# Block sums of k as two more columns of its transposing products, the last output tile in two halves, and a new listing: block-sparse attention followed by an MLP-mixer

## The chip, the core and the metric

The kernel runs on one NeuronCore of a Trainium2 chip. The core has a matrix engine (TensorE, PE; its weight loads are shown apart as PEld), a vector engine (VectorE, DVE), an activation engine (ScalarE, ACT), a general engine (GpSimd, POOL) and a queue engine that issues transfers (SyncE, SP). Each engine takes its instructions strictly in the order in which they are listed, and waits where an input or a buffer isn't ready. The metric is the device time of one execution in microseconds; the median of several runs counts.

## The reference

```python
# q, k, v: (4, 8, 768, 64); block = 64, n_blocks = 12, top_k = 3
k_rep = k.reshape(B, H, n_blocks, block, D).mean(axis=3)
gate_scores = np.einsum('bhsd,bhnd->bhsn', q, k_rep)
gate_scores = np.where(causal, gate_scores, -1e9)     # causal by blocks
top_idx = np.argsort(gate_scores, axis=-1)[..., -top_k:]
# a query attends to the blocks in top_idx and to its own, causally
scores = scale * np.matmul(q, k.transpose(0, 1, 3, 2))
attn = softmax(np.where(mask, scores, -1e9))
x = np.matmul(attn, v)                                # heads side by side: (4, 768, 512)
# the mixer, x as (batch, token, channel)
h = np.maximum(x.T @ w_tok1, 0.0) @ w_tok2            # along the tokens, 768 -> 256 -> 768
u = x + h.T
out = u + np.maximum(u @ w_ch1, 0.0) @ w_ch2          # along the channels, 512 -> 1536 -> 512
```

Which three blocks a query takes depends on comparisons of gate scores, so these are computed more exactly than the rest, which is in 16 bits.

## The kernel before, in words

The 32 heads are handled as 16 pairs, 0 to 15; four pairs make a batch. `pair(p)` writes down the steps of one pair, `mlp(b)` those of a batch's channel MLP. No step is issued there: each goes into a planner (`Plan`) with its engines and estimated costs, the buffers that it reads and writes, and a due time `pr`, made of the pair's start and a constant of the table `L` (lines 46 to 51). `Plan.run` then lists the steps for each engine, always taking the ready step with the earliest due time, chooses between engines where a step may run on two, and assigns ring buffers; that listing is what the engines follow. Where it sees PE idle before the first MLP, it puts in products of zeros (`fill`, L766).

Steps of a pair, with their lines:

- k, q and v are loaded by SP (L472, L477) into rings of three buffers each.
- k's six tiles of 128 keys x two heads are transposed on PE in f32, by products with the identity `id32` (`transposed`, L419), in two halves of three tiles, each into one of four PSUM tiles `pm`. ACT or DVE copies them in f16 to KA (`kev`, L496).
- Block sums of k: pairs 0 to 3 take them with a reduction on DVE over the transposed half in PSUM (L487), which leaves six sums per half; a product with `side` (L491) spreads them into `ks2`, the two heads apart. Pairs 4 to 7 reduce in the same way and split the sums in three bf16 parts (L433, L436). Pairs 8 to 15 transpose k in f16 (L508) and get the sums from a separate load of k (`block_sums`, L444, L449).
- q is transposed likewise and copied to QT (`qev`), and from there cast to QA on one of three engines.
- The gate: PE multiplies q with the sums, in f32 for pairs 0 to 3 (L543), in bf16 parts for the others (L559, L526, L552). DVE adds the causal bias (L546, L564), finds the third largest of each row (L573, L575), compares (L576) and masks the own block (L579) into `bn`. For pairs 0 to 4 PE transposes these bits (L598) and ACT or DVE copies them into QA's last 12 rows; for pairs 5 to 15 DVE transposes them (L584) and four transfers on SP carry them there (L587).
- Scores (L619): QA against KA, whose last 12 rows hold the block indices, so that the mask comes out of the product itself. The scores go into two PSUM tiles `sc`, in three pieces per head; ACT takes the exponential (L626), POOL cuts the diagonal blocks (L634), PE multiplies with v (L643), DVE divides (L646, L650).
- The mixer along the tokens: L661, a rectification, L675, an addition on DVE (L678), a transpose to uT (L686 and copies).

The channel MLP of a batch runs in two halves of 384 tokens: 12 groups of four products (`ch1`, L704) with a rectification each (L710 on ACT or L712 on DVE), then three output tiles of 128 tokens x 512 channels, 12 products each (`ch2`, L721), an addition on DVE (L724) and a write of 256 KB by SP (L727). Its products stand between the attention steps of later batches.

Of the kernel before, what the change touches and what calls it, by code (L numbers as in the profile page):

```python
# [9 lines left out]
FP = mybir.dt.float32  # L10
# [3 lines left out]
ALU = mybir.AluOpType  # L14
AX = mybir.AxisListType
# [9 lines left out]
def _layout():  # L25
    col, diag, width = {}, [], []
    for g, banks in enumerate(GROUPS):
        mine, w = [], 0
        for bk, pieces in enumerate(banks):
# [13 lines left out]
COL, DIAG, WIDTH = _layout()  # L43

EARLYP = 8
EARLY, PACE = 5.58, 13.33
L = dict(kd=28.57, qd=25.92, vd=11.57, va=-8.52, kt=12.35, kr=17.84, ke=-10.79, qt=15.5, qe=4.07, q16=14.86, g=19.74,
         b=14.78, k16=23.05, kx=14.61, kc=15.1, r=24.94, kb=35.09, ks=47.26, w1=2.86, w2=-1.57, wc1=17.92, wc2=28.28,
         tok=9.0, ml=12.54, o0=-0.3, o1=1.07, o2=2.31, o3=0.96, o4=-4.5, o5=1.61, o6=-2.0, o7=-4.89, o8=-4.68,
         o9=0.71, o10=0.86, o11=-1.11, o12=-2.65, o13=-2.86, o14=1.45, o15=0.65, m0=-2.18, m1=-0.36, m2=-0.52,  # L50
         m3=-1.94, th=3.11, bd=4.29)


class Ring:
# [187 lines left out]
def dve(n, rate=0.96):  # L242
    return {"DVE": (n / rate + 70.0, n / rate + 155.0)}
# [15 lines left out]
def kernel(  # L259
# [33 lines left out]
    def sb(shape, dt, name):  # L293
        return sp.tile(shape, dt, tag=name, name=name)
# [4 lines left out]
    def copy(e, out, in_):  # L299
        if e is nc.scalar:  # L300
            e.copy(out=out, in_=in_)  # L301
        else:
            e.tensor_copy(out=out, in_=in_)  # L303

    P = Plan()
    ENG = {"PE": nc.tensor, "ACT": nc.scalar, "DVE": nc.vector, "POOL": nc.gpsimd, "SP": nc.sync}
# [19 lines left out]
    w1 = sb([128, NJ, DT], F16, "w1")  # L326
# [28 lines left out]
    nc.vector.memset(zero, 0.0)  # L355
    nc.gpsimd.memset(id32, 0.0)
    nc.gpsimd.affine_select(out=id32, in_=id32, pattern=[[-1, 128]], compare_op=ALU.not_equal, fill=1.0, base=0, channel_multiplier=1)
    nc.gpsimd.memset(ind, MASKV)
    nc.gpsimd.affine_select(out=ind, in_=ind, pattern=[[1, S]], compare_op=ALU.is_ge, fill=0.0, base=0, channel_multiplier=-64)
    nc.gpsimd.affine_select(out=ind, in_=ind, pattern=[[-1, S]], compare_op=ALU.is_ge, fill=0.0, base=63, channel_multiplier=64)  # L360
# [56 lines left out]
    def transposed(src, i, t):  # L417
        for j in range(3):
            nc.tensor.transpose(out=t[:, 128 * j:128 * j + 128], in_=src.t[:, 3 * i + j].rearrange("p x d -> p (x d)"), identity=id32)  # L419

    def halves(i):
        return slice(HS * i, HS * i + HS)
# [38 lines left out]
    def pair(p):  # L461
# [2 lines left out]
        step = T(p + 1) - T(p)  # L464
        t0 = T(p) + L[f"o{p}"]
        early, thirds = p < FIRST, p >= L["th"]
        q32, k32, v32 = Buf(q32r), Buf(k32r), Buf(v32r)
        qs, ks_, vs = q[b, h:h + 2], k[b, h:h + 2], v[b, h:h + 2]
        QA, KA, VA, QT = Buf(QAr), Buf(KAr), Buf(VAr), Buf(QTr)
# [11 lines left out]
        if early:  # L481
            ks2b = kp = Buf(kppr if thirds else ksr)
            ks3 = Buf(ks3r) if thirds else None
            for i in range(2):
                t = Buf(Rr)
                P.op(pe(slow=3), lambda t=t, i=i: transposed(k32, i, t.t), rd=[(k32, 0), (k32, 1)], wr=[(t, 0)], pr=t0 - L["kt"])
                P.op(dve(HS), lambda t=t, i=i: nc.vector.tensor_reduce(  # L487
                    out=ks3.t[:, 0, 6 * i:6 * i + 6] if thirds else t.t[:, HS:HS + 6], in_=t.t[:, 0:HS].rearrange("c (n w) -> c n w", w=64),
                    axis=AX.X, op=ALU.add), rd=[(t, 0)], wr=[(ks3, i) if thirds else (t, 1)], pr=t0 - L["kr"])
                if not thirds:  # L490
                    P.op({"DVE": (150.0, 220.0)}, lambda t=t, i=i: nc.vector.tensor_tensor(  # L491
                        out=ks2b.t[:, :, 6 * i:6 * i + 6], in0=t.t[:, HS:HS + 6].rearrange("c (o n) -> c o n", o=1).broadcast_to([128, 2, 6]),
                        in1=side, op=ALU.mult), rd=[(t, 1)], wr=[(ks2b, i)], pr=t0 - L["kr"] + 0.1)
                for x in range(2):
                    def kev(e, t=t, i=i, x=x):
                        copy(ENG[e], KA.t[0:64, x, halves(i)], t.t[64 * x:64 * x + 64, 0:HS])  # L496
                    P.op({**dve(HS), **act(HS)}, kev, rd=[(t, 0)], wr=[(KA, (x, i))], pr=t0 - L["ke"])
            if thirds:
                split(ks3, lambda x: kp.t[64 * x:64 * x + 64, :, x, :], lambda h, x: h[64 * x:64 * x + 64], [(ks3, 0), (ks3, 1)], kp, t0 - L["kr"] + 0.1)
        else:  # L500
            k16 = Buf(k16r)
            P.op({"POOL": (840.0, 880.0)}, lambda: nc.gpsimd.tensor_copy(
                out=k16.t, in_=k32.t.rearrange("p j x d -> p j (x d)")), rd=[(k32, 0), (k32, 1)], wr=[(k16, 0)], pr=t0 - L["k16"])
            t = Buf(Rr)

            def ktr(t=t):
                for j in range(NJ):
                    nc.tensor.transpose(out=t.t.bitcast(F16)[:, 128 * j:128 * j + 128], in_=k16.t[:, j, :], identity=id16)  # L508
            P.op(pe(*[128] * NJ), ktr, rd=[(k16, 0)], wr=[(t, 0)], pr=t0 - L["kt"])
            for x in range(2):  # L510
                def kev(e, t=t, x=x):
                    copy(ENG[e], KA.t[0:64, x, :], t.t.bitcast(F16)[64 * x:64 * x + 64, 0:S])
                P.op({"DVE": (530.0, 610.0), **act(S)}, kev, rd=[(t, 0)], wr=[(KA, (x, 0)), (KA, (x, 1))], pr=t0 - L["ke"])
# [58 lines left out]
                for x in range(2):  # L572
                    nc.vector.max(out=m8.t[:, j, x, :], in_=gm.t[:, j, NB * x:NB * x + NB])  # L573
        P.op({"DVE": (730.0, 820.0)}, top, rd=[(gm, 0)], wr=[(m8, 0)], pr=t0 - L["g"] + 0.2)
        P.op({"DVE": (140.0, 210.0)}, lambda: nc.vector.tensor_copy(out=third(), in_=m8.t[:, :, :, 2:3]), rd=[(m8, 0)], wr=[(g, 1)], pr=t0 - L["g"] + 0.25)  # L575
        P.op({"DVE": (220.0, 300.0)}, lambda: nc.vector.tensor_tensor(  # L576
            out=below(), in0=gm.t.rearrange("p j (x n) -> p j x n", n=NB), in1=third().broadcast_to([128, NJ - 1, 2, NB]), op=ALU.is_lt),
            rd=[(gm, 0), (g, 1)], wr=[(g, 0)], pr=t0 - L["g"] + 0.3)
# [114 lines left out]
    def mlp(b):  # L693
        u, uT = u_of[b], uT_of[b]
        t0, span = T(PPB * (b + 1)) + L["ml"] + L[f"m{b}"], PACE * PPB
        n = 0
        for i in range(2):
            h2 = Buf(h2r)
            for f in range(NFC):
                m = Buf(Rr, "mlp")  # L700

                def ch1(f=f, i=i, m=m):
                    for c in range(NCC):
                        nc.tensor.matmul(out=m.t[:, 0:HS], lhsT=wc1[:, c, 128 * f:128 * f + 128], rhs=uT.t[:, c, HS * i:HS * i + HS],  # L704
                                         start=(c == 0), stop=(c == NCC - 1))
                P.op(pe(*[HS] * NCC), ch1, rd=[(uT, (c, i)) for c in range(NCC)] + [W["wc1", c] for c in range(NCC)], wr=[(m, 0)], pr=t0 + span * n / 48)

                def relu(e, f=f, m=m, h2=h2):
                    if e == "ACT":
                        nc.scalar.activation(out=h2.t[:, f, :], in_=m.t[:, 0:HS], func=AF.Relu)  # L710
                    else:
                        nc.vector.tensor_scalar(out=h2.t[:, f, :], in0=m.t[:, 0:HS], scalar1=0.0, scalar2=None, op0=ALU.max)  # L712
                P.op({**act(HS), **dve(HS)}, relu, rd=[(m, 0)], wr=[(h2, f)], pr=t0 + span * n / 48 + 0.05)
                n += 1
            for jj in range(3):
                j = 3 * i + jj
                m, o = Buf(Rr, "mlp"), Buf(osr)
                for s in range(4):
                    def ch2(jj=jj, s=s, m=m, h2=h2):
                        for f in range(3 * s, 3 * s + 3):  # L720
                            nc.tensor.matmul(out=m.t, lhsT=h2.t[:, f, 128 * jj:128 * jj + 128], rhs=wc2[:, f, :], start=(f == 0), stop=(f == NFC - 1))  # L721
                    P.op(pe(*[DM] * 3), ch2, rd=[(h2, f) for f in range(3 * s, 3 * s + 3)] + [W["wc2", 3 * s]], wr=[(m, 0)], pr=t0 + span * n / 48)
                    n += 1
                P.op(dve(DM), lambda j=j, m=m, o=o: nc.vector.tensor_tensor(  # L724
                    out=o.t.rearrange("p (c d) -> p c d", d=128), in0=u.t[:, :, j, :], in1=m.t.rearrange("p (c d) -> p c d", d=128), op=ALU.add),
                    rd=[(m, 0)] + [(u, (c, i)) for c in range(NCC)], wr=[(o, 0)], pr=t0 + span * n / 48 + 0.05)
                P.op({"SP": (600.0, 1500.0, 700.0)}, lambda j=j, o=o: nc.sync.dma_start(out=out[b, 128 * j:128 * j + 128, :], in_=o.t),  # L727
                     rd=[(o, 0)], wr=[(o, 0)], pr=t0 + span * n / 48 + 0.06)

    for b in range(B):  # L730
        if b * PPB >= FIRST:
# [78 lines left out]
```

## Time and profile before

| what | value |
|---|---|
| three runs | 264.1, 264.17, 264.48 us; median 264.17 |
| profiled execution | 264.49 us, of which 262.8 us are the span from the first to the last instruction |
| busy PE, PEld | 250.4 us (95%), 172.1 us (65%) |
| busy DVE, ACT, POOL | 157.3 us (60%), 167.1 us (64%), 120.0 us (46%) |
| granted clock of TensorE | 0.998 |
| moved by DMA | 33.21 MB |

A busy time is the union of an engine's instructions; a product's end is modelled, so products that overlap in the pipeline count once. In a row of the timeline or the chain stand the start in us, the duration in us, the engine, the line, and what is written from what; "x6" is a run of six. In a row of groups stand the count, the busy time in us and the mean of one in ns, then the idle time before them and what ended it. In a row by stage stands the stretch, then per engine the busy time and the number of instructions, the granted clock, the mean busy share of the DMA engines and GB/s.

### The profile page before, as it was taken

To read this page: it belongs to the slowest core of one execution; us is meant where nothing else is said; L and a number is where in the kernel's file an instruction comes from. 1 tells how busy PE (TensorE), PEld (TensorE's weight loads), DVE (VectorE), ACT (ScalarE), POOL (GpSimd) and SP (SyncE) were. 2 spreads that over 40 slices of the span, in tenths; PEclk is the share of its full clock that TensorE was granted. 3 is DMA by queue.
4 is the path that set the end of the run, shared out by engine and by line. 5 is a ranking of instruction groups with operands and counts; after the bars stand their busy time and mean duration, and the time that the engine had idled before them with its cause. 6 is when DMAs were issued, how large, how long until landed. Compare 5 with 4: busy or idle time off the path is not lost.

```text
span 262.8 us, 6757 instructions
## 1 busy us (share of the span) xinstructions
PE 250.4 (95%) x2585; PEld 172.1 (65%) x2585; DVE 157.3 (60%) x527; ACT 167.1 (64%) x265; POOL 120.0 (46%) x222
## 2 busy tenths in 40 slices
PE   7689999988999999999999999999999999999994
PEld 7566688775667677666776677657665665554541
DVE  5788997998368475786684767638574452301103
ACT  2689989975776683459974968457765661360520
POOL 8136884963256898666993807133132110000000
PEclk9999999999999999999999999999999999999999
DMA  8999997689998799943997940021002100212103
GB/s 165 224 211 215 231 221 148 102 139 146 179 269 139 190 246 220 241 85 126 213 219 158 216 114 2 8 80 42 7 2 75 54 0 2 80 40 80 44 0 120
DMA packets 88960, 33.21 MB, mean 126 GB/s; under 512 B 82464, under 2 KB 85152, under 8 KB 88736
## 3 DMA queue, kind: packets, MB, share of 16 engines
q1 hardware_dynamic: 83984, 28.33, 50.0%
q0 software_dynamic: 3232, 3.93, 9.8%
q10 hardware_dynamic: 1712, 0.52, 1.0%
q8 instruction: 20, 0.33, 0.5%
q14 instruction: 12, 0.10, 0.1%
HBM read 30.01 MB, written 6.29 MB: 138 GB/s over the span
## 4 chain that ended last, share of the span: by engine, by line
PE 83%; DVE 6%; DMA 4%; ACT 2%; issue 2%; SPq 1%; DVEq 0%; ACTq 0%
PE pm L704 20%; PE pm L721 18%; PE sc L619 12%; PE pm L643 7%; PE sc L721 5%; PE pm L419 4%; PE pm L661 4%; PE pm L675 3%; PE sc L704 3%; PE pm L559 2%; DMA k<-in_k_dram 2%; DMA QA<-bnt 2%; PE pm L686 2%; ACT E L626 1%; PE pm L508 1%
## 5 line engine op out<-in xcount | busy, mean ns | idle before, releaser
L626 ACT ACTIVATE E<-sc 128x1024 f16<-128x1024 f32 (+1 forms) x96 | 83.7, 918 | 13.8 <-PE sc L619 12.7
L634 POOL TENSOR_SCALAR_AFFINE_SELECT E<-E 128x256 f16<-128x256 f16 x96 | 38.8, 409 | 69.1 <-ACT E L626 68.6
L704 PE MATMUL pm<-uT,wc 128*128 128x384 f16 x340 | 64.3, 326 | 0.0
L721 PE MATMUL pm<-wc,h 128*128 128x512 f16 x228 | 59.2, 379 | 0.0
L704 PEld LDWEIGHTS <-wc 128*128 128x128 f16 x384 | 36.2, 98 | 23.2 <-issue 0.6
L619 PE MATMUL sc<-QA,KA 76*128 76x512 f16 (+3 forms) x256 | 49.0, 305 | 2.0 <-DMA QA<-bnt 1.1
L710 ACT ACTIVATE h<-pm 128x384 f16<-128x384 f32 x60 | 29.5, 492 | 20.9 <-PE pm L704 20.7
L721 PEld LDWEIGHTS <-h 128*128 128x128 f16 x288 | 26.6, 98 | 23.3 <-issue 1.0
L619 PEld LDWEIGHTS <-KA 76*128 76x128 f16 x256 | 22.8, 98 | 16.7 <-issue 2.9
L643 PEld LDWEIGHTS <-E 128*128 128x128 f16 x672 | 25.1, 98 | 4.9 <-issue 1.1
L643 PE MATMUL pm<-VA,E 128*128 128x65 f16 x651 | 25.5, 193 | 1.0 <-ACT uT L301 0.9
L724 DVE TENSOR_TENSOR os<-u,pm 128x512 f32<-128x512 f16 x19 | 12.9, 681 | 20.5 <-PE pm L721 19.1
L712 DVE TENSOR_SCALAR h<-pm 128x384 f16<-128x384 f32 x25 | 13.9, 555 | 13.1 <-PE pm L704 12.7
L449 POOL TENSOR_TENSOR kb<-kb 96x512 f32<-96x512 f32 (+2 forms) x18 | 20.0, 1114 | 0.0
L303 POOL CAST QA<-QT 64x768 f16<-64x768 f32 x12 | 9.8, 819 | 20.7 <-ACT QT L301 18.7
L724 DVE TENSOR_TENSOR os<-u,sc 128x512 f32<-128x512 f16 x5 | 3.3, 686 | 26.0 <-PE sc L721 26.0
L650 DVE TENSOR_TENSOR x<-pm,rc 128x384 f16<-128x384 f32 x31 | 17.2, 556 | 0.8
L678 DVE TENSOR_TENSOR u<-x,pm 128x384 f16<-128x384 f16 x30 | 15.5, 547 | 2.7 <-PE pm L675 2.5
L301 ACT COPY uT<-pm 128x384 f16<-128x384 f16 x21 | 9.1, 486 | 12.5 <-PE pm L686 12.5
L301 ACT COPY QT<-pm 128x384 f32<-128x384 f32 x24 | 11.0, 485 | 8.0 <-PE pm L419 7.8
L552 POOL TENSOR_TENSOR R<-R 128x640 bf16<-128x640 f32 x12 | 15.0, 1252 | 1.9 <-DVE R L526 0.9
L419 PE MATMUL pm<-id,q 128*128 128x128 f32 x96 | 14.6, 276 | 1.0 <-ACT QT L301 1.0
(90 smaller groups left out, 358.0 us busy)
## 6 DMA issues: line engine op xcount, KB each, us to landing
k<-in_k_dram SPq DMA_DIRECT2D x32, 192.0 KB
v<-in_v_dram SPq DMA_DIRECT2D x16, 384.0 KB
out_dram<-os SPq DMA_DIRECT2D x24, 256.0 KB
q<-in_q_dram SPq DMA_DIRECT2D x30, 192.0 KB
wc<-in_moe_w_ch_dram POOLq DMA_DIRECT2D x8, 384.0 KB, 6.3
kb<-in_k_dram SPq DMA_DIRECT2D x2, 1536.0 KB
w<-in_moe_w_tok_dram POOLq DMA_DIRECT2D x2, 384.0 KB, 6.2
QA<-bnt SPq DMA_DIRECT2D x44, 9.0 KB
```

Source lines behind the costliest of these rows:

```text
L301: e.copy(out=out, in_=in_)
L419: nc.tensor.transpose(out=t[:, 128 * j:128 * j + 128], in_=src.t[:, 3 * i + j].rearrange("p x d -> p (x d)"), identity=id32)
L449: P.op({"POOL": (step * 2.15 + 60, step * 2.15 + 140)}, lambda n=n, o=o, step=step: nc.gpsimd.tensor_tensor(out=kb.t[:, o:o + step] if n > ...
L619: nc.tensor.matmul(out=s.t[:, at:at + 128 * m], lhsT=KA.t[:, x, 128 * kk:128 * kk + 128], rhs=QA.t[:, q0:q0 + m, x, :], start=True, stop=True)
L626: nc.scalar.activation(out=E.t[:, 1024 * g_:1024 * g_ + WIDTH[g_]], in_=s.t[:, 0:WIDTH[g_]], func=AF.Exp, scale=scale)
L634: nc.gpsimd.affine_select(out=o, in_=o, pattern=[[0, 2], [1, 128]], compare_op=ALU.is_ge, fill=0.0, base=0, channel_multiplier=-1)
L643: nc.tensor.matmul(out=t[:, jq, :], lhsT=E.t[:, cc:cc + 128], rhs=VA.t[:, x, kk, :], start=(kk == 0), stop=(kk == jq))
L650: P.op(dve(384), lambda a=a, rc=rc, x=x: nc.vector.tensor_tensor(out=xp.t[:, :, 64 * x:64 * x + 64], in0=a.t[:, 0:NJ * 65].rearrange("p (j ...
L704: nc.tensor.matmul(out=m.t[:, 0:HS], lhsT=wc1[:, c, 128 * f:128 * f + 128], rhs=uT.t[:, c, HS * i:HS * i + HS], start=(c == 0), stop=(c == ...
L710: nc.scalar.activation(out=h2.t[:, f, :], in_=m.t[:, 0:HS], func=AF.Relu)
L721: nc.tensor.matmul(out=m.t, lhsT=h2.t[:, f, 128 * jj:128 * jj + 128], rhs=wc2[:, f, :], start=(f == 0), stop=(f == NFC - 1))
L724: P.op(dve(DM), lambda j=j, m=m, o=o: nc.vector.tensor_tensor(out=o.t.rearrange("p (c d) -> p c d", d=128), in0=u.t[:, :, j, :], in1=m.t.r ...
```

## The change

Three things. First, for pairs 0 to 3 the identity gets two more columns, ones in the upper and in the lower 64 rows (`idk`, 128 x 130, set up on POOL). k's tiles are multiplied with it by ordinary f32 products, so that each tile of 128 keys comes out transposed with its two block sums beside it, and the reductions fall away; the product with `side` reads the sums from their columns. Pairs 4 to 7 keep the reductions. Second, the last output tile of the last batch is made in two halves of 256 channels, each with its own products, addition and write. Third, the table `L` and `PACE` have new values, so that the planner lists everything anew.

```diff
-EARLY, PACE = 5.58, 13.33
+EARLY, PACE = 5.58, 12.85
...
+    idk = sb([128, 130], FP, "idk")
+    nc.gpsimd.memset(idk, 0.0)
+    nc.gpsimd.affine_select(out=idk[:, 0:128], in_=idk[:, 0:128], pattern=[[-1, 128]], compare_op=ALU.not_equal, fill=1.0, base=0, channel_multiplier=1)
+    for x in range(2):
+        nc.gpsimd.memset(idk[64 * x:64 * x + 64, 128 + x:129 + x], 1.0)
...
+        sums = p < L["sm"] and not thirds
...
+                if sums:
+                    def turned(t=t, i=i):
+                        for j in range(3):
+                            nc.tensor.matmul(out=t.t[:, 130 * j:130 * j + 130], lhsT=k32.t[:, 3 * i + j].rearrange("p x d -> p (x d)"), rhs=idk, start=True, stop=True)
+                    P.op(pe(slow=6), turned, rd=[(k32, 0), (k32, 1)], wr=[(t, 0)], pr=t0 - L["kt"])
                     P.op({"DVE": (150.0, 220.0)}, lambda t=t, i=i: nc.vector.tensor_tensor(
-                        out=ks2b.t[:, :, 6 * i:6 * i + 6], in0=t.t[:, HS:HS + 6].rearrange("c (o n) -> c o n", o=1).broadcast_to([128, 2, 6]),
-                        in1=side, op=ALU.mult), rd=[(t, 1)], wr=[(ks2b, i)], pr=t0 - L["kr"] + 0.1)
+                        out=ks2b.t[:, :, 6 * i:6 * i + 6].rearrange("c x (j n) -> c x j n", n=2),
+                        in0=t.t[:, 0:390].rearrange("c (o j w) -> c o j w", o=1, w=130)[:, :, :, 128:130].broadcast_to([128, 2, 3, 2]),
+                        in1=side.rearrange("c x (j n) -> c x j n", n=2), op=ALU.mult), rd=[(t, 0)], wr=[(ks2b, i)], pr=t0 - L["kr"])
...
-                m, o = Buf(Rr, "mlp"), Buf(osr)
+                o = Buf(osr)
+                wide = DM // 2 if b == B - 1 and j == NJ - 1 else DM
+                for w in range(0, DM, wide):
+                    m = Buf(Rr, "mlp")
...
```

The copies to KA read the transposed tiles at a stride of 130 columns for these pairs. In the new listing there is more that differs: on SP the loads of k for pair 3 stand ahead of v for pair 0, and those of k for pair 4 ahead of q for pair 2; the bits of pair 5 are transposed sooner behind their gate; ten groups of `ch1` for seven stand ahead of pair 5's scores; and for pairs 12 to 15 less of PE's other work stands between a pair's gate and its first scores.

More of the change, by code (lines that the diff above doesn't have):

```diff
@@ L494, in pair @@
                 for x in range(2):
                     def kev(e, t=t, i=i, x=x):
-                        copy(ENG[e], KA.t[0:64, x, halves(i)], t.t[64 * x:64 * x + 64, 0:HS])
+                        a = t.t[64 * x:64 * x + 64]
+                        copy(ENG[e], KA.t[0:64, x, halves(i)].rearrange("d (j w) -> d j w", w=128),
+                             a[:, 0:390].rearrange("d (j w) -> d j w", w=130)[:, :, 0:128] if sums else a[:, 0:HS].rearrange("d (j w) -> d j w", w=128))
                     P.op({**dve(HS), **act(HS)}, kev, rd=[(t, 0)], wr=[(KA, (x, i))], pr=t0 - L["ke"])
@@ L574, in pair @@
         P.op({"DVE": (730.0, 820.0)}, top, rd=[(gm, 0)], wr=[(m8, 0)], pr=t0 - L["g"] + 0.2)
-        P.op({"DVE": (140.0, 210.0)}, lambda: nc.vector.tensor_copy(out=third(), in_=m8.t[:, :, :, 2:3]), rd=[(m8, 0)], wr=[(g, 1)], pr=t0 - L["g"] + 0.25)
+        P.op({"DVE": (165.0, 240.0)}, lambda: nc.vector.tensor_copy(out=third(), in_=m8.t[:, :, :, 2:3]), rd=[(m8, 0)], wr=[(g, 1)], pr=t0 - L["g"] + 0.25)
         P.op({"DVE": (220.0, 300.0)}, lambda: nc.vector.tensor_tensor(
@@ L716, in mlp @@
                 j = 3 * i + jj
-                m, o = Buf(Rr, "mlp"), Buf(osr)
[L718 to L728, printed above, removed]
+                o = Buf(osr)
```

38 lines of the change are left out of this document (28 added, 10 removed).

## The prediction

> **What bounds the kernel now.** I read the busy time by stage first, then the chain that ended last, then the timelines of VectorE (DVE) and TensorE (PE) in the first stage, then single groups.
>
> ```profile
> core 0: us, PE busy (x) PEld busy (x) DVE busy (x) ACT busy (x) POOL busy (x), PEclk, DMA share, GB/s
> 6.40:59.00 52.60, 47.23 (x632) 38.76 (x633) 45.98 (x177) 46.33 (x72) 31.84 (x63) 1.00 1.04 187
> 59.00:65.20 6.20, 5.11 (x49) 3.25 (x48) 5.50 (x23) 2.96 (x7) 2.42 (x7) 1.00 1.01 141
> 65.20:215.00 149.80, 149.80 (x1595) 102.32 (x1594) 93.26 (x304) 102.17 (x157) 79.49 (x133) 1.00 0.59 127
> 215.00:262.80 47.80, 43.56 (x267) 23.15 (x264) 8.89 (x15) 14.17 (x30) 0.81 (x2) 0.99 0.14 50
> ```
>
> From 65.2 to 215 us PE has no idle time at all: that stage is bound by PE's own work, and PE does the same work there in either kernel. What can change lies elsewhere: 5.4 us (52.60 - 47.23) of PE idleness up to 59 us, where PE, ACT and DVE are each near 90% busy and wait for one another; 1.1 us (6.20 - 5.11) behind it; and the end after PE's last product.
>
> ```profile
> 20.40 1.03 PE pm L543 x10
> ...
> 22.38 0.68 PE pm L419 x6
> ...
> 59.47 4.73 DMA QA<-bnt
> 64.33 1.03 PE sc L619 x6
> ...
> 259.08 0.69 DVE os L724
> ```
>
> These are rows of the chain: start, time, what. Pair 5's scores (L619) at 64.33 wait for a transfer of gate bits that was issued from 56.29 on; that is the 1.1 us. At the end one addition on DVE of 0.69 us stands behind the last product, and a write of 256 KB behind it.
>
> **The block sums, in the first stage.** Removed: eight DVE reductions, two per pair of pairs 0 to 3.
>
> ```profile
> L487 DVE TENSOR_REDUCE pm<-pm 128x6 f32<-128x384 f32 x8 | 4.5, 558 | 0.9 <-PE pm L419 0.8
> L543 PE MATMUL pm<-ks,QT 128*128 128x24 f32 x40 | 4.9, 264 | 1.2 <-DVE ks L491 1.2
> L543 PEld LDWEIGHTS pm<-ks,QT 128*128 128x128 f32 x40 | 4.8, 192 | 1.6 <-ACT QT L301 1.5
> L365 POOL MEMSET side<- 64x6 f32 x2 | 0.5, 273 | 0.1
> L357 POOL TENSOR_SCALAR_AFFINE_SELECT id<-id 128x128 f32<-128x128 f32 x1 | 0.3, 292 | 0.1
> ```
>
> The 24 transposes of k become 24 ordinary f32 products with 130 columns. A transposing step costs 113 ns (0.68 us for 6, chain). No row shows the new one. From below: the gate's f32 product, which the trace records in two parts, takes 206 ns (1.03 us for 5) with only 24 columns; two parts of a transpose's length make 226 ns. From above: if the gate's 206 is weight loading that can't hide behind the columns, 226 + 206 = 432 ns. I take 226, since loads overlap with products elsewhere in this trace (PEld is busy beside PE in every stage). That adds 24 x 0.113 = 2.7 us to PE's work, all before 25 us.
>
> The Trainium skill ("FP8 and Floating Point Precision", TensorE Precision Notes) says that a true FP32 product makes four passes through the array; with 130 columns at the 2.4 GHz of its page "TensorE: Matmul & The Clock Gate" that is an estimate of 217 ns, 0.2 us less in the sum; the trace's 206 ns at 24 columns doesn't fall with the columns as four passes would, so it speaks for loading as the floor there.
>
> What the reductions cost where they stand:
>
> ```profile
> 3.85 2.68 DVE L379 COPY KA<-ind 12x768 f16<-12x768 f16 x6 [1.72 <-POOL ind L360]
> ...
> 10.63 0.28 DVE L546 TENSOR_TENSOR gm<-pm,cst 128x120 f32<-128x120 f32 x1 [0.92 <-issue]
> 10.95 0.82 DVE L573 MAX8 m<-gm 128x8 f32<-128x12 f32 x10
> 11.68 0.55 DVE L487 TENSOR_REDUCE pm<-pm 128x6 f32<-128x384 f32 x1
> 12.14 0.17 DVE L575 COPY pm<-m 128x10 f32<-128x10 f32 x1
> 12.22 0.56 DVE L487 TENSOR_REDUCE pm<-pm 128x6 f32<-128x384 f32 x1
> 12.68 0.28 DVE L576 TENSOR_TENSOR pm<-gm,pm 128x120 f32<-128x120 f32 x1
> ...
> 13.06 0.28 DVE L579 TENSOR_TENSOR bn<-pm,cst 128x120 f16<-128x120 f32 x1
> ...
> 14.15 1.00 DVE L303 COPY QA<-pm 12x640 f16<-12x640 f16 x2 [0.33 <-PE pm L598]
> 16.86 3.66 ACT L626 ACTIVATE E<-sc 128x1024 f16<-128x1024 f32 x4
> ```
>
> Two of them, 0.46 us each from start to start, sit in pair 0's own gate chain. I walked the new listing by hand: each instruction starts when its engine is free and its inputs are there, 0.2 us after a PE group for the engine that evicts it, 0.05 us otherwise, with these durations. Pair 0's gate product stays at 9.25: its k products end 0.7 us later (six at 0.226 for six at 0.113) and push q's transposes, which cancels the reductions saved ahead of the gate. The setup of the 130-column identity puts about 1 us on POOL ahead of the index rows (a select like the old identity's, 0.29, a memset no longer than that, and two memsets at 0.27), and so the KA copies on DVE, which wait for those rows, end near 7.5 for 6.53 (3.85 + 2.68); DVE's first new input comes at 7.96, so this is hidden; with that cover gone it costs up to 1 us. Then pair 0's bits are done at 12.5 for 13.3, its QA rows at 14.2 for 15.15, its first exponential starts at 15.95 for 16.86.
>
> **The new listing of the first stage** gives part of this back and takes it again later. The loads of k for pair 3 go ahead of q for pair 2 on SP's queue, and of v for pair 0.
>
> ```profile
> 16.22 0.49 PE L419 MATMUL pm<-id,q 128*128 128x128 f32 x3
> ...
> 20.24 1.19 PE L543 MATMUL pm<-ks,QT 128*128 128x24 f32 x10
> ...
> 59.01 1.46 PE L704 MATMUL pm<-uT,wc 128*128 128x384 f16 x8
> 56.29 3.95 SPq L587 DMA_DIRECT2D QA<-bnt  x4
> ```
>
> Pair 2's q is transposed at 16.22 now; in the walk it waits for a PSUM tile until 21.4, and its gate comes at 24.4 for 20.24. Queued behind it on PE stand pair 1's second scores, for which ACT waits: the thirteenth exponential starts 1.0 us later than now. Behind it the order is better: the thirtieth ends at 52.55, the gate bits of pair 5 leave DVE without two evictions between them (their transfer is issued at 54.7 for 56.29), and the first MLP product, ahead of which both listings put the same PE work, starts at 58.05 for 59.01. I take -0.9 us. Bounds: the walk's own worst lag is 1.6 us (the twenty-first exponential), so +1.6 at the least favourable; at best PE's 5.4 us of idleness swallow the 2.7 us of new work and vanish, -2.7.
>
> **59 to 65 us.** Ten groups of L704 stand ahead of pair 5's scores for seven. The bits landed 64.33 - 56.29 = 8.0 us after the first issue; issued at 54.7 they land at 62.7, and the scores are due at 65.4: the wait of 1.1 us goes, -1.1. If the transfer is slower by 2.7 us it comes back; it can't gain more.
>
> **65 to 215 us.** There is no idleness to win, only to lose. Per pair the chain is: gate product, DVE steps, bnt transposed, four issues on SP, landing, scores. PE must have other work as long as this takes.
>
> ```profile
> 181.25 0.23 PE L559 MATMUL pm<-ksp,R 128*128 128x72 bf16 x2
> 184.60 0.57 DVE L584 STREAM_TRANSPOSE bnt<-bn 128x384 f16<-128x384 f16 x1
> 185.23 3.31 SPq L587 DMA_DIRECT2D QA<-bnt  x4
> 189.00:189.50 0.50, 0.50 (x6) 0.30 (x4) 0.41 (x1) 0.29 (x1) 0.00 (x0) 1.00 0.16 19
> 189.50:190.00 0.50, 0.50 (x6) 0.48 (x5) 0.00 (x0) 0.34 (x2) 0.00 (x0) 1.00 0.00 0
> 194.45 0.23 PE L559 MATMUL pm<-ksp,R 128*128 128x72 bf16 x2
> 198.17 0.58 DVE L584 STREAM_TRANSPOSE bnt<-bn 128x384 f16<-128x384 f16 x1
> 205.51 0.60 PE L619 MATMUL sc<-QA,KA 76*128 76x512 f16 x3
> ```
>
> Here it takes 3.3 us to bnt, 0.6 to the issue, 4.3 until the last packets stopped (189.5): 8.2 us; for the next pair 3.7 + 0.6 + 4.3 = 8.6, and its scores come at 205.51, 11.0 us behind its gate, without a wait. Counting the work listed between gate and first scores at the rows' paces, pairs 12 to 15 have 11.3, 11.2, 11.0 and 11.0 us now, and 8.3, 8.2, 7.8 and 9.3 in the new listing. With 8.2 us PE waits 0.4 in all, with 8.6 it waits 0.3 + 0.4 + 0.8 = 1.5. I take +0.7; from below nothing, from above as in the second rival.
>
> **The last tile in halves.** PE's work is the same columns in twice as many products.
>
> ```profile
> 259.80:260.50 0.70, 0.00 (x0) 0.00 (x0) 0.00 (x0) 0.00 (x0) 0.00 (x0) 1.00 0.00 0
> 260.50:261.50 1.00, 0.00 (x0) 0.00 (x0) 0.00 (x0) 0.00 (x0) 0.00 (x0) 0.99 0.70 262
> 261.50:262.80 1.30, 0.00 (x0) 0.00 (x0) 0.00 (x0) 0.00 (x0) 0.00 (x0) 0.50 0.00 0
> ```
>
> The listing interleaves the halves' products, so the first is ready only 0.3 us (three of 256 columns) ahead; its addition, half of 0.69 and some fixed part, say 0.42, is in the way of the second's. DVE ends 0.58 us behind PE's last product for 0.78, -0.2. The write moves its 262 KB within 1.0 us (260.5 to 261.5); half of it is half that, and the first half's has begun 0.4 us before, -0.4 after rounding down. Together -0.6; bounds 0 (the second write waits for the first) and -0.85 (0.35 + 0.5).
>
> By the Trainium skill ("DMA: Bandwidth & Descriptors", Anatomy of one DMA) most of a DMA is a fixed 2.0 us and its bytes pass at 436 GB/s; the trace agrees as to the fixed part (0.7 + 1.3 us of no packets), and by the skill's rate half the write saves 0.3, not 0.5.
>
> **The sum.** -0.9 - 1.1 + 0.7 - 0.6 = -1.9 us. The profiled execution took 264.49 us (span 262.8 and 1.7 around it), the top of the three runs; the median is 264.17. So 264.17 - 1.9 = 262.3.
>
> **The rivals.**
> 1. The f32 products cost 432 ns (slower). Fifteen of them stand ahead of the first scores (pairs 0 and 1 and half of pair 2), 15 x 0.206 = 3.1 us on the path, the others in ACT's shadow: -1.9 + 3.1 = +1.2, 265.4. It decides from 0.226 + 1.9/15 = 353 ns on. For it: f32 loads take 192 ns in the group's row; against it: 226 already holds two parts.
> 2. The gate bits come late in pairs 12 to 14 (slower). If DVE, which has evictions listed ahead of those chains, begins each 1 us later than in the quoted pair, 9.6 us are needed: 1.3 + 1.4 + 1.8 = 4.5 us of PE standing still instead of 0.7: +1.9, 266.1. It passes no change where the need exceeds 9.0 us (0.7 + 0.8 + 1.2 = 2.6). For it: nothing else hides PE there; against it: the two quoted pairs need 8.2 and 8.6.
> 3. Pair 2's late q costs all that the reductions give, and pair 5's wait moves along: only the end and the 0.7 remain, +0.1, 264.3, no change. For it: the walk is 1.6 us behind in the middle.
> 4. PE's idleness vanishes as far as it can: -2.7 - 1.1 - 0.6 = -4.4, 259.8.
>
> **Chances.** Forecast 0.45, rivals 0.12, 0.13, 0.20, 0.10. The forecast's own range is 261.0 to 263.6; with the others 260.2 to 265.6. What a measurement can tell is 0.2%, 0.53 us. Faster: the forecast (0.43), rival 4, and 0.05 of rival 3: 0.58. Same: 0.02 and half of rival 3: 0.12. Slower: rivals 1 and 2 and 0.05 of rival 3: 0.30.
>
> **What would show it.** The group of the new k products with starts 226 ns apart in a run of three (432: rival 1). The first exponential near 16, the first product of L722 (now L704) near 58, pair 5's scores without a wait for a DMA. PE idle under 1.5 us in all between 65 and 215, its waits naming QA<-bnt at pairs 12 to 14. The span ending 3.2 us behind PE's last product for 3.8. The forecast is wrong if the first MLP product comes after 59.5, or if PE stands still over 2.6 us in the long stage.

## The result, and the profile after

The changed kernel takes 265.31 us at the median of 22 runs (264.38 to 268.17), the kernel before 264.25 in the same session: ratio 1.0054, 95% interval [1.0032, 1.0076]. It is slower by about 1.1 us; 1.9 us faster had been forecast. Each run lists TensorE's mean granted clock, and the changed kernel's runs fall apart by it: thirteen at 0.998 or above with a median of 265.03, nine at 0.987 to 0.994 with 266.0 to 268.2. Medians "at full clock" below are those of runs at 0.997 or above; the kernel before has 264.1 to 264.3 there in each of the later sessions, so that the changed kernel is 0.8 us slower at full clock. The kernel before has lower clocks too, in 2 of 19, 13 of 25, 8 of 20 and 4 of 20 runs of those sessions; executions more than 1.5% above the fastest of the same kernel are left out of these counts and of the ratios. The profiled execution took 266.95 us and is one of the nine.

By stage (stretch, busy time per engine with instruction counts, granted clock, DMA share, GB/s), the changed kernel:

```profile
core 0: us, PE busy (x) PEld busy (x) DVE busy (x) ACT busy (x) POOL busy (x), PEclk, DMA share, GB/s
6.40:59.00 52.60, 49.96 (x643) 42.03 (x644) 44.12 (x171) 44.78 (x67) 29.39 (x63) 0.97 1.06 194
59.00:65.20 6.20, 6.09 (x63) 4.22 (x61) 3.92 (x10) 4.30 (x10) 5.09 (x9) 1.00 0.67 104
65.20:215.00 149.80, 148.07 (x1575) 100.41 (x1574) 90.99 (x310) 103.45 (x158) 80.33 (x133) 1.00 0.59 126
```

The wait before 65 us is gone (6.09 busy of 6.20), but the long stage, which had none, has 1.73 us of PE idleness (149.80 - 148.07). The steps named beforehand, from the timelines of PE and ACT:

```profile
15.41 1.03 PE L637 MATMUL sc<-QA,KA 76*128 76x512 f16 x6
16.04 2.75 ACT L644 ACTIVATE E<-sc 128x1024 f16<-128x1024 f32 x3 [0.51 <-PE sc L637]
16.28 1.50 PE L495 MATMUL pm<-idk,k 128*128 128x130 f32 x12
17.62 0.44 PE L637 MATMUL sc<-QA,KA 76*128 76x512 f16 x2
...
60.12 0.81 PE L722 MATMUL pm<-uT,wc 128*128 128x384 f16 x4
```

Six k products (two records each) take 17.62 - 16.28 = 1.34 us, 223 ns each. The first exponential starts at 16.04 for 16.86. The first MLP product comes at 60.12 for 59.01, and one reason is the clock:

```profile
30.00:31.00 1.00, 0.57 (x6) 0.33 (x4) 0.97 (x6) 0.95 (x3) 1.00 (x3) 0.93 1.46 202
31.00:34.00 3.00, 3.00 (x28) 2.37 (x29) 2.35 (x16) 2.29 (x4) 1.73 (x3) 0.50 1.26 236
34.00:35.00 1.00, 1.00 (x22) 0.82 (x21) 0.74 (x3) 1.00 (x2) 1.00 (x2) 0.86 0.97 206
```

For 3.4 us PE is granted half its clock. PE's waits in the long stage (us in total, times, longest), the timelines of DVE, SP and PE around pair 11, then of PE at pair 14:

```profile
PE sc L637 <- DMA QA<-bnt: 1.6, 3, 1.1
```

```profile
142.65 0.57 DVE L602 STREAM_TRANSPOSE bnt<-bn 128x384 f16<-128x384 f16 x1
...
143.15 2.06 SPq L750 DMA_DIRECT2D out_dram<-os  x1
145.30 3.31 SPq L605 DMA_DIRECT2D QA<-bnt  x4
...
147.51 1.46 PE L722 MATMUL pm<-uT,wc 128*128 128x384 f16 x8
150.03 1.03 PE L637 MATMUL sc<-QA,KA 76*128 76x512 f16 x6 [1.06 <-DMA QA<-bnt]
...
194.62 0.83 PE L679 MATMUL pm<-x,w 128*128 128x128 f16 x12
195.71 1.03 PE L637 MATMUL sc<-QA,KA 76*128 76x512 f16 x6 [0.26 <-DMA QA<-bnt]
```

Pair 11's bits are transposed by 143.2, but their transfers are issued from 145.3 on: SP is held by the write ahead of them. The figure in brackets counts from the modelled end of the product before, and the loss is larger: the eight products from 147.51 on start 0.162 us apart, so PE could have begun the scores at 148.81 and loses 1.22 us. At the end (PE and DVE), with the last tile's products in the kernel before on top:

```profile
256.24 2.75 PE L721 MATMUL pm<-wc,h 128*128 128x512 f16 x12
```

```profile
258.52 0.49 PE L742 MATMUL pm<-wc,h 128*128 128x256 f16 x3
...
258.77 0.69 DVE L746 TENSOR_TENSOR os<-u,sc 128x512 f32<-128x512 f16 x1
...
259.52 0.49 PE L742 MATMUL sc<-wc,h 128*128 128x256 f16 x3 [0.51 <-DVE os L746]
...
261.48 0.49 PE L742 MATMUL sc<-wc,h 128*128 128x256 f16 x3
```

The halves need two PSUM tiles; the second's is that of the fifth output tile, free when DVE has read it. Groups of three start 0.33 us apart, so 259.52 instead of 258.85 is a loss of 0.67 us.

### The profile page after: what moved, and what is told of

It is laid out like the page before. It is cut to its first block, busy times and chain, and to the rows that moved or that the text cites. A ratio compares the mean times of both kernels' runs of the same rounds, so it can differ in the third digit from the quotient of the medians.

```text
span 265.2 us, 6807 instructions
## 1 busy us (share of the span) xinstructions
PE 255.5 (96%) x2619; PEld 177.5 (67%) x2619; DVE 151.2 (57%) x516; ACT 171.1 (65%) x268; POOL 121.3 (46%) x227
## 4 chain that ended last, share of the span: by engine, by line
PE 83%; DVE 6%; SPq 4%; DMA 3%; POOL 2%; issue 1%; ACT 0%; DVEq 0%; POOLq 0%
PE pm L722 19%; PE pm L742 15%; PE sc L637 13%; PE pm L661 7%; PE sc L742 5%; PE pm L424 4%; PE pm L679 3%; SPq L605 3%; PE pm L693 3%; PE sc L722 3%; DMA QA<-bnt 3%; PE pm L495 2%; PE pm L577 2%; PE pm L704 2%; DVE KA L303 1%; PE pm L561 1%
## 5 line engine op out<-in xcount | busy, mean ns | idle before, releaser
L722 PE MATMUL pm<-uT,wc 128*128 128x384 f16 x332 | 62.4, 326 | 0.0
L742 PE MATMUL pm<-wc,h 128*128 128x512 f16 (+1 forms) x228 | 58.6, 373 | 0.0
L637 PE MATMUL sc<-QA,KA 76*128 76x512 f16 (+3 forms) x256 | 50.3, 309 | 2.1 <-DMA QA<-bnt 1.6
L742 PEld LDWEIGHTS <-h 128*128 128x128 f16 x300 | 27.8, 98 | 22.8 <-issue 0.8
L728 ACT ACTIVATE h<-pm 128x384 f16<-128x384 f32 x56 | 27.5, 490 | 17.8 <-PE pm L722 17.6
L746 DVE TENSOR_TENSOR os<-u,pm 128x512 f32<-128x512 f16 (+1 forms) x19 | 12.7, 668 | 29.0 <-PE pm L742 28.9
L661 PE MATMUL pm<-VA,E 128*128 128x65 f16 x672 | 27.0, 195 | 0.0
L742 PE MATMUL sc<-wc,h 128*128 128x512 f16 (+1 forms) x72 | 17.7, 361 | 0.5 <-DVE os L746 0.5
L544 DVE TENSOR_TENSOR R<-pm,QT 128x256 f32<-128x256 f32 (+1 forms) x24 | 11.0, 486 | 10.2 <-ACT QT L301 7.6
L301 ACT CAST QA<-QT 64x768 f16<-64x768 f32 x18 | 14.9, 829 | 0.4
```

The source lines that it names most:

```text
L637: nc.tensor.matmul(out=s.t[:, at:at + 128 * m], lhsT=KA.t[:, x, 128 * kk:128 * kk + 128], rhs=QA.t[:, q0:q0 + m, x, :], start=True, stop=True)
L661: nc.tensor.matmul(out=t[:, jq, :], lhsT=E.t[:, cc:cc + 128], rhs=VA.t[:, x, kk, :], start=(kk == 0), stop=(kk == jq))
L742: nc.tensor.matmul(out=m.t[:, 0:wide], lhsT=h2.t[:, f, 128 * jj:128 * jj + 128], rhs=wc2[:, f, w:w + wide], start=(f == 0), stop=(f == NFC ...
```

## The experiments

Times are medians at full clock, with the number of such runs; "SP" is its queue of transfers.

**Which part costs? One part alone in the listing of before.** First the sums:

```diff
-    P.op(pe(slow=3), lambda ...: transposed(k32, i, t.t), ...)
+    # turned(): 130-column products with idk, as in the change; reduction left out
+    P.op(pe(slow=3), turned, ...)
```

> The kernel before in its own listing, with only the k products of pairs 0 to 3 made with the 130-column identity and the reductions gone. Theory A (the sums by themselves win in the first stage): 0.3 to 1.2 us below the kernel before, first exponential about 0.9 us sooner (15.9 to 16.0 for 16.86), nothing changed behind 65 us; the slower time of the changed kernel is then the new listing's. Rival B (the 2.7 us of PE's new work cost): 0.3 to 1.5 us above the kernel before. Should the granted clock fall here as in the changed kernel, the listing is not its cause.

265.28 us (12 runs), ratio 1.0023 [1.0002, 1.0045], never a lower clock: 1.1 us slower than the 264.16 of before at full clock. Rival B holds. PE there, and ACT, then PE in the kernel before:

```profile
13.45 0.47 PE L611 MATMUL pm<-id,bn 128*64 128x128 f16 x5
13.85 1.61 PE L495 MATMUL pm<-idk,k 128*128 128x130 f32 x12
15.29 1.19 PE L556 MATMUL pm<-ks,QT 128*128 128x24 f32 x10
16.32 0.59 PE L632 MATMUL sc<-QA,KA 76*128 76x512 f16 x3
...
16.96 3.66 ACT L639 ACTIVATE E<-sc 128x1024 f16<-128x1024 f32 x4
```

```profile
13.64 0.47 PE L598 MATMUL pm<-id,bn 128*64 128x128 f16 x5
14.04 0.87 PE L419 MATMUL pm<-id,k 128*128 128x128 f32 x6
14.75 1.19 PE L543 MATMUL pm<-ks,QT 128*128 128x24 f32 x10
15.79 0.59 PE L619 MATMUL sc<-QA,KA 76*128 76x512 f16 x3
```

What the gate chain saves is lost again on PE's queue: k products twice as long stand between pair 0's bits and its scores, which come 0.5 us later, not sooner; the first exponential starts at 16.96 for 16.86, where 0.9 us sooner had been expected.

The same work without the saving:

```diff
-    nc.tensor.transpose(out=t[:, 128 * j:128 * j + 128], in_=k32..., identity=id32)
+    nc.tensor.matmul(out=t.t[:, 128 * j:128 * j + 128], lhsT=k32..., rhs=id32, start=True, stop=True)
```

> The kernel before in its own listing; k's tiles of pairs 0 to 3 are multiplied with the plain identity by ordinary f32 products (128 columns, about 222 ns) in place of transposes, and the reductions stay. It has the PE work of the new products (2.6 us) without what they save. With the sums made the new way in this listing the time was 1.1 us above the kernel before. Theory A (the removed reductions save a part in the same listing, because they stand in pair 0's and pair 1's gate chains): 1.5 to 2.2 us above the kernel before, so the reductions were worth 0.4 to 1.1. Rival B (DVE's reductions lie beside other work and their removal saves nothing here): 0.9 to 1.3 us above. Beside this, if transposes are what lets the granted clock fall, no run here has a mean clock below 0.997, as with the 130-column products.

266.22 (4 runs; three more had clocks of 0.991 to 0.994), 2.0 us over the 264.26 of before. So the work costs 2.0 and the removed reductions give about 0.9 back: theory A. As to the clock its expectation failed: products in place of transposes did not keep it up. In the profiled run it fell near 11 us, not near 31 as in the changed kernel (granted clock 0.50):

```profile
11.00:14.00 3.00, 3.00 (x15) 2.94 (x16) 1.11 (x11) 0.95 (x2) 0.00 (x0) 0.50 1.31 221
```

The last tile alone, its halves one after the other:

```diff
+    late = [second half's four groups]; first = [first half's four groups]
+    order = [o for o in order if o not in late]
+    at = order.index(first[-1]) + 1
+    order[at:at] = late
```

> The kernel before in its own listing, with only the last output tile in two halves, the second half's products behind the first's. Theory A: the last addition and write are half as long: 0.5 to 0.7 us from DVE and the write, no wait for a PSUM tile; median 0.4 to 0.8 us below the kernel before. Rival B (the write's fixed time and a second issue on SP take it back): within 0.2 us.

263.72 (7 runs) for 264.16, 0.4 us faster at full clock; the ratio over the runs at every clock, 0.9989 [0.9965, 1.0013], would not tell it from nothing. Both edits together:

> The sums of pairs 0 to 3 and the last tile in two sequential halves, both in the listing of the kernel before. If both parts are worth what I gave them, they add to 0.8 to 1.9 us: 262.3 to 263.4 us, and the new listing alone made the change slower. If only the halves count, 263.4 to 263.9; if the sums cost more than they save, 264.2 or more.

264.53 (12 runs): the halves take 0.75 off the sums' 265.28, and the two together are still 0.4 us slower than before, the last of the three cases expected.

**Is the new listing the cost?** The new table with the block sums the old way, planned anew; and the sums undone in the new listing as it stands:

```diff
-    th=3.11, bd=4.29, sm=5.39)
+    th=3.11, bd=4.29, sm=0)
```

```diff
-    nc.tensor.matmul(out=t.t[:, 130 * j:130 * j + 130], lhsT=k32..., rhs=idk, ...)
+    nc.tensor.transpose(out=t.t[:, 130 * j:130 * j + 128], in_=k32..., identity=id32)
...
+    nc.vector.tensor_reduce(...)   # straight ahead of the product with side
```

> The changed kernel with the block sums the old way for all pairs, planned anew with the new table: the table and the last tile's halves without the new products. By the runs so far, at full clock: kernel before 264.2, plus the sums alone 265.3, the sums, sequential halves and the new listing 264.1; so the new listing itself looks worth -0.4. Theory A (the new table suits only the shorter chain of the new sums): first stage 0.5 to 1.5 us later than in the changed kernel's full-clock runs though PE has 2.7 us less to do, 265 to 267 us, and runs with the clock below 0.99 where products of zeros no longer fill PE's gaps. Rival B (PE's 2.7 us of work is the whole cost of the change): 262.3 to 263.5 us.

> The changed kernel in its own listing, with the block sums of pairs 0 to 3 taken the old way: transposes by the plain identity, and the eight reductions on DVE, each straight ahead of its product with the masks. It tells what the new k products are worth where the rest is the same. Theory A (my sum: 24 products at 226 for 113 ns cost PE 2.7 us, mostly hidden, and the reductions' 0.46 us each stand in DVE's way): first exponential 0.6 to 1.0 us later than the changed kernel's 15.9, first product of L722 0 to 0.9 us later; median 0.3 to 1 us above the changed kernel's at equal clock. Rival B (PE's added 2.7 us is what costs): 0.5 to 1.5 us below it. Beside this, if the f32 transposes and gates let the clock fall, it should do so here in as many runs or more, since the transposing products of k are back to transposes; if it was the new products, never.

267.5 in the one full-clock run, 269.7 over all six; and 270.86 over six runs, none at full clock (0.967 to 0.981), so that neither theory of the second could be judged at equal clock. In it the clock was at half for ten microseconds:

```profile
13.00:23.00 10.00, 9.28 (x48) 7.23 (x49) 6.42 (x27) 5.57 (x10) 2.35 (x4) 0.50 1.11 206
```

So the new table gains nothing without the new sums (2.4 us over the changed kernel in that one run, in a listing that was planned anew), and how much of the second kernel's time is the clock stays open. The sums do better in the new listing than in the old: with sequential halves they stand at 264.08 (next) and at 264.53.

**The tail**, the move of the halves made in the changed kernel:

> The changed kernel with one move: in the last output tile the four groups of products of the second half stand behind all four of the first half, not between them. Theory A: in the profile of the changed kernel PE stands 0.67 us near 259.5 because the second half's first product needs a PSUM tile that the previous tile's addition on DVE frees only then; with the move the first half's products (about 1.3 us) cover that. PE's standing still behind 215 us falls by 0.5 to 0.7 us, the first half's addition and write start about 1 us before the last product, median 0.5 to 0.8 us below the changed kernel's in the same runs of the clock (264.5 to 264.8 at full clock). Rival B: the end is set by the last write's fixed time and DVE, and the product order changes less than 0.2 us.

264.08 (10 runs), 0.95 below the changed kernel, more than the 0.67 seen as a wait; the two ran in different sessions. The profiled run had the full clock, so that its first MLP product shows what the first stage takes without the fall. PE's last two rows are now without a gap:

```profile
58.31 0.81 PE L723 MATMUL pm<-uT,wc 128*128 128x384 f16 x4
...
256.54 1.47 PE L743 MATMUL pm<-wc,h 128*128 128x256 f16 x12
257.85 1.47 PE L743 MATMUL sc<-wc,h 128*128 128x256 f16 x12
```

**The long stage**, by SP's order:

```diff
+    for p, back in ((10, [q loads of pair 13]), (11, [write of batch 1's second tile])):
+        moved behind the four bit transfers of pair p
```

> The changed kernel with two moves on SP's queue alone: the two loads of q of pair 13 go behind the four transfers of pair 10's gate bits, and the write of batch 1's second output tile behind the four of pair 11's. Theory A (PE's waits of 0.49 us at 134 and 1.22 us at 148.6 come from the bits standing ready while SP is held by the transfer ahead): both waits go, PE's idle time from 65.2 to 215 us falls from 1.73 to 0.2 to 0.5 us, median 1.2 to 1.6 us below the changed kernel's at equal clock (263.4 to 263.8 at full clock). Rival B (the four small transfers are slow by themselves, behind the traffic on the rings, whatever SP issues before them): the idle time stays above 1.2 us and the median within 0.4 us. Rival C: the moved q load or write becomes late for its own reader, and a wait of like size appears at pair 13 or at the output ring.

264.37 (8 runs), 0.66 below the changed kernel: between theory A and rival B. Pair 10's wait is gone, pair 11's is not (the profiled run was one at 0.987). SP's rows and PE's waits:

```profile
142.63 1.27 SPq L484 DMA_DIRECT2D v<-in_v_dram  x2
143.99 5.37 SPq L606 DMA_DIRECT2D QA<-bnt  x4
```

```profile
PE sc L638 <- DMA QA<-bnt: 1.3, 2, 1.1
```

Pair 11's four issues take 5.4 us, straight behind two loads of v, for 3.3 in the changed kernel. With those and the write behind the bits, and the halves in sequence (SP's row and the stage row):

```diff
+    i = sp.index(first bit transfer of pair 11)
+    sp[i - 3:i] (v, v, write) moved behind the four bit transfers of pair 11
```

> The changed kernel with the last tile's halves one after the other, and three more transfers moved on SP's queue than in the first try: besides the two loads of q of pair 13 behind pair 10's gate bits, the two loads of v and the write that stood straight ahead of pair 11's bits now stand behind them. In the first try pair 10's wait was gone but pair 11's stayed at 1.1 us, and the four issues of its bits took 5.4 us on SP for 3.3 elsewhere: the issue itself was held up, behind two loads of v listed 1.4 us before. Theory A (the rows issued just before fill what the queue can hold, so bits issued behind a pause are quick): the four issues take 3.3 to 3.5 us, pair 11's wait falls below 0.3 us, PE's idle time from 65.2 to 215 us is 0.2 to 0.6 us, median at full clock 262.7 to 263.3, 0.8 to 1.4 us below the version that has only the halves moved (264.1). Rival B (pair 11's bits are late for another reason, the transpose on DVE or the landing): wait above 0.8 us, 263.8 to 264.3.

```profile
140.87 3.32 SPq L606 DMA_DIRECT2D QA<-bnt  x4
```

```profile
65.20:215.00 149.80, 149.47 (x1592) 101.57 (x1590) 91.04 (x300) 104.93 (x159) 81.39 (x136) 1.00 0.57 123
```

263.24 (6 runs; ratio to before over the runs at every clock 0.9969 [0.9937, 1.0001]), PE idle 0.33 us in the stage: theory A. Run again (262.68 for 264.06, 7 runs, ratio 0.9963 [0.9928, 0.9998]) it is the fastest version found, at full clock 1.0 and 1.4 us faster than the kernel before in the same sessions.

**59 to 65 us alone**: two MLP groups moved in the kernel before, with sequential halves.

```diff
+    at = order.index(first scores of pair 5)
+    order[at:at] = the two groups of ch1 that stood behind them
```

> The kernel before in its own listing with the last tile in two sequential halves, and two groups of the first MLP product (four products each) moved ahead of pair 5's first scores, where PE stands 1.09 us for the gate bits. It tests the 59 to 65 us term of the prediction by itself. Theory A: the wait is covered and PE, which has no idle time behind it, ends that much sooner: 0.8 to 1.1 us below the version with the halves alone, 262.6 to 263.0 us at full clock, faster than both kernels. Rival B: the exponentials behind the later scores (0.3 to 0.5 us) push the waits on, and less than 0.4 us is left: 263.3 to 263.8.

```profile
62.51 2.77 PE L705 MATMUL pm<-uT,wc 128*128 128x384 f16 x16
65.11 1.03 PE L620 MATMUL sc<-QA,KA 76*128 76x512 f16 x6
66.89 0.43 PE L620 MATMUL sc<-QA,KA 76*128 76x512 f16 x2 [0.74 <-ACT E L627]
```

263.87 (3 runs) for 263.72: nothing gained. The first wait went, and the next scores wait 0.74 us for an exponential that started later: rival B, and worse. (The profiled run was one at 0.994; its clock fell near 11 us.)

**The clock.** Products of zeros ahead of two gates; these with the tail's and SP's moves (the first of the two); zeros only where PE stands idle:

```diff
+    for _ in range(16): nc.tensor.matmul(out=g.t[:, 392:512], lhsT=zero, rhs=zero[:, 0:120], ...)   # ahead of the gates of pairs 2 and 3
...
+    ZEROS = {(3, 1): 10, (4, 0): 9}   # behind these halves of q
```

> The changed kernel with 16 products of zeros (128 x 120, f16, about 0.05 us each, 0.8 us in all) in front of the gate products of pairs 2 and 3; their results are overwritten or never read. The profiled execution of the changed kernel shows TensorE's granted clock at 0.50 from about 31 to 34.2 us, and its 22 runs fall in two groups, nine with a mean clock of 0.994 (266.0 to 268.2 us) and thirteen near 1.0 (264.4 to 265.7). Theory A (the clock falls because PE does little but f32 transposes and narrow f32 gates, with gaps, from 27 to 31 us, and other products in that stretch prevent it): no run with a mean clock below 0.997, every run within 264.6 to 265.8 us, median 265.0 to 265.4 (up to 0.8 us of the added work is not hidden). Rival B (the fall has nothing to do with what PE executes there): clock 0.994 in about two runs of five as before, and the median 0 to 1.6 us above the changed kernel's 265.3.

> The three edits together: zeros ahead of two gates, the last tile's halves one after the other, and the two moves on SP's queue. If the three losses are separate they add: no run below clock 0.997, PE's idle time in the long stage at most 0.5 us, about 0.6 us less at the end, so 262.8 to 263.5 us, faster than the kernel before by 0.8 to 1.4 us (ratio 0.995 to 0.997). If the losses only move (another pair's bits late, another wait at the end), 263.9 to 264.8.

> The version with sequential halves and the five transfers moved, plus 19 products of zeros (128 x 120, f16, about 0.05 us each) in the two places shortly before 31 us where PE stands idle: ten behind pair 3's second half of q (idle 0.38 us before the next scores) and nine behind the first half of pair 4's q (idle 0.43 us). Without them 6 of 12 runs had a mean clock of 0.987 to 0.994 (263.8 to 265.9 us), the others 263.2 at the median. Theory A (idle time on PE before 31 us is what lets the clock fall): no run below 0.997, median 263.0 to 263.4. Rival B (the f32 transposes and narrow f32 gates in that stretch let it fall, whether or not PE idles between them): low clock in 3 to 7 of 12 runs, as often as in the version without the zeros on the same chip. Rival C: the zeros delay the scores and the gate behind them, +0.3 to 0.8 us in all runs.

The first: 267.49, all 5 at full clock, but 2.5 us over the changed kernel: the zeros stand in PE's way. Its clock held although a pause of 0.38 us was left ahead of the second batch of zeros:

```profile
28.53 0.43 PE L641 MATMUL sc<-QA,KA 76*128 76x512 f16 x2 [0.38 <-ACT E L648]
28.86 1.00 PE L563 MATMUL pm<-zero 128*128 128x120 f16 x16
```

The three edits: 265.25, all 6 at full clock; above both ranges expected; the losses did not add up to a gain. With the idle places filled (19 zeros), 12 of 12 runs at full clock; the same kernel without them, as the control on the same chip:

> The version with sequential halves and the five transfers moved once more, as the control on the same chip for the one with the added zeros, since how often the clock falls may differ between chips. By either theory: full-clock runs at 262.9 to 263.5 us, a lower clock in a quarter to a half of the runs.

5 of its 12 runs were at 0.987 to 0.994. So the added products keep the clock up, as theory A forecast and rival B did not, though rival C holds beside it with more than its 0.8 us: 263.79 for 262.68, because q's eviction now waits behind the zeros (DVE's row), and the gate behind the eviction:

```profile
27.24 0.69 PE L542 MATMUL pm<-zero 128*128 128x120 f16 x10
...
28.03 0.56 DVE L304 COPY QT<-pm 128x384 f32<-128x384 f32 x1 [0.53 <-PE pm L542]
28.65 1.29 PE L567 MATMUL pm<-ks,QT 128*128 128x24 f32 x10 [0.43 <-DVE QT L304]
```

The pause of 0.38 us has become one of 0.43 us ahead of this gate. That idleness by itself lets the clock fall is therefore not shown: in this kernel PE is busy for less of the stretch below than of the one ahead of the changed kernel's fall (2.87 of 3.40 us), and no run of it fell.

```profile
52.70:56.10 3.40, 2.66 (x48) 2.39 (x48) 3.23 (x19) 2.10 (x6) 2.26 (x4) 1.00 0.75 120
```

What PE does there differs as well: mostly f16 products here, f32 transposes and f32 gates ahead of the fall. No run separates the two.

## Why the prediction was wrong, step by step

- **226 ns a product**: 223. Rival 1 is out; that its time, 265.4 us, lies near the measured one is chance.
- **First stage, -0.9**: the right size. With a full clock (the version with only the halves moved) the first MLP product comes at 58.31 for 59.01, -0.7. PE's idleness up to 59 us falls from 5.37 to 2.75 us there (52.60 - 49.85), which takes up nearly all of the new work. But the reason that I gave, a shorter gate chain with PE's 2.7 us "mostly hidden", holds for the new listing alone; in the old one PE's work cost 2.0 us and the chain gave about 0.9.
- **59 to 65 us, -1.1**: came true in this listing, 6.09 of 6.20 us busy. That it is worth its whole wait wherever it is removed did not hold in the old listing, where the wait only moved (3 runs).
- **65 to 215 us, +0.7**: the failed step. PE's idleness is 1.73 us by the stage row, most of it at pairs 10, 11 and 14. Counted from start to start in the trace, each product against the median spacing of its form, the loss is 2.7 us, for 0.13 in the kernel before: 0.49 us ahead of pair 10's scores, 1.22 ahead of pair 11's, 0.25 and 0.43 ahead of those of pairs 13 and 14, and 0.3 in smaller pieces. So the term was right for the pairs that it counted, 12 to 15 (0.68), and left out pairs 10 and 11 (1.71). I took 0.6 us from `bnt` to the first issue on SP, read at two pairs late in the stage where nothing stood ahead. At pair 11 it was 145.30 - 142.65 = 2.65 us, behind a write, at pair 10 130.00 - 127.71 = 2.29 us, behind two loads of q. The bits are late as in rival 2, but at other pairs, and held by SP, not by DVE. What the diff moved on SP was in the listing; I used it for the early loads only. Moving five transfers on SP's queue brought 0.84 us back (263.24 for 264.08). (The 2.6 us at which rival 2 is said to pass no change add up to 2.7 from their three terms.)
- **The end, -0.6**: the second failed step. Behind PE's last product it came true: the span ends 265.2 - 261.97 = 3.2 us behind it, as forecast, for 3.8. But I let the halves' products alternate without asking which PSUM tile the second gets, and the wait of 0.67 us eats all of it: from the last tile's first product to the end it is 6.7 us (from 258.52) for 6.6 (from 256.24). The section of the Trainium skill that the prediction names at this term ("DMA: Bandwidth & Descriptors", Anatomy of one DMA) describes transfers issued by GpSimd; these writes are issued by SP, and the 2.0 us without packets are the trace's own.
- **What no step had**: the granted clock. It was 1.00 in every stage row that I read but the last. It makes the difference between 265.03 and the median of 265.31, and 1 to 3 us in single runs.

At full clock, and from start to start: -0.7 up to the first MLP product, -1.3 for the wait before 65 us, +2.6 in the long stage, -0.3 from 215 to 240 us (0.52 us lost for 0.84), +0.3 behind that (0.95 us lost for 0.10, 0.6 gained behind the last product) = +0.6, for +0.8 measured. The 0.2 that is left is less than the 0.3 us by which the profiled execution of the kernel before lies above its median (264.49 and 264.17).

## What to carry to other kernels

Where one engine is busy for 95% of the span, work moved onto it has to be paid for unless it lands in idle time that nothing else would fill: price it with the work alone and the saving alone (2.0 us of 2.7, and 0.9, here). When a listing changes, read what stands ahead of each small, urgent transfer on its issuing queue, at every place where it is issued, not at the quietest. The output cut in two gained here with its parts one after the other (0.4 us) and not with their products alternating, when the second part had no free accumulator. And read a wait from start to start, since a modelled end hides a part of it.

## What was unexpected in the hardware

The clock fell to one half after stretches in which PE was only partly idle. Before the fall PE was busy 2.87 of 3.40 us in the changed kernel, with two pauses of some 0.4 us; 19 to 32 short f16 products of zeros in that stretch and shortly before it ended the falls, in all 23 runs of three kernels:

```profile
27.30:30.70 3.40, 2.87 (x23) 2.09 (x22) 3.26 (x9) 3.38 (x5) 3.06 (x6) 1.00 1.35 237
```

The Trainium skill ("TensorE: Matmul & The Clock Gate", Part 1) describes a free-running window of about 3.4 us over which activity is judged; the half clock here lasted 3.4 us, which agrees, and a window that runs free would explain why it falls in some runs and not in others. In the trace of the first try on SP's queue it lasted 6.8 us and with the sums undone 10.2 us, two and three times as long. The Trainium skill's rule to avoid idle gaps of about 3 us (same page, Why this matters for your kernels) would have let this case pass: all idle time of that stretch together is 0.53 us. Its Part 4 says that transposes don't count as busy in the same way; the runs don't settle that. With ordinary products in place of k's transposes 3 of 7 runs still had lower clocks, but in the profiled one the clock fell at another place, behind a stretch in which PE was busy only 2.16 of 3.40 us (7.0 to 10.4 us) with q's transposes still in it; and the zeros helped with all transposes of q in place.

An f32 product of 130 columns takes hardly longer (223 ns) than one of 24 (206 ns). Four small transfers took 3.3 us to issue behind a pause, and at one place 5.4 us behind two loads of v that had been issued in 1.3 us; behind two loads of q that had themselves taken 2.2 us (pair 10 in the changed kernel) they took 3.3 again.
